# Batch 0's attention of a fused attention and max-out kernel, rewritten over both token halves

## The chip, the cores and the metric

The kernel runs on one core of one Trainium2 chip. The metric is device time in microseconds (us). The kernel before takes 320.83 us, the median of three runs (320.79 to 321.07). One execution was recorded by the hardware profiler; its own numbers are below.

## The reference

There are 8 batches of 8 heads, 1024 tokens and 64 values per head. Keys and values are first projected along the tokens, from 1024 rows to 64, by the matrices E and F. Then ordinary softmax attention follows, and its output goes through a max-out layer.

```
k_proj = np.einsum('ks,bhsd->bhkd', E, k)          # 64 x 64 per head
v_proj = np.einsum('ks,bhsd->bhkd', F, v)
scores = scale * np.matmul(q, k_proj.transpose(0, 1, 3, 2))
attn   = exp(scores) / sum(exp(scores))
x      = np.matmul(attn, v_proj)                   # -> 8192 tokens x 512
out    = np.maximum(x @ w1, x @ w2) @ w_out        # 512 -> 1024 -> 512
```

Inputs and output are float32. Because max(a, b) = max(a - b, 0) + b, the kernel computes `relu(x @ (w1 - w2)) @ w_out + x @ (w2 @ w_out)`. The difference `w1 - w2` is called `wd_sb`, the product `w2 @ w_out` is called `m_sb`.

## The kernel before, in words

Everything is float16 on the chip, with float32 sums. Each batch is cut into two token halves of 512 columns, and these are the units of work; there are 16. The order of the instructions is written out by hand: every engine works through its instructions in the order of the program text, and waits only where a semaphore says so. TensorE (PE) does the products, VectorE (DVE) and ScalarE (ACT) take results out of PSUM, GpSimd (POOL) issues the loads that change float32 to float16 on their way, and SyncE (SP) issues stores, transposing transfers and the first few plain loads.

The change touches the start of the kernel, that is batch 0 up to the point where the max-out products run without a break. The start of the program text is as follows.

- **Loads.** SP issues E (L80), then k of heads 0 and 1 as plain float32 (`kf_sb`, L81), then F (L82). POOL issues, each with a change of type: k of heads 2 and 3, then it makes the identity matrix, then q of heads 0 to 3, k of heads 4 to 7, q of heads 4 to 7 (all L102), v in four pieces of two heads (L102), and then the weights. The first four weight pieces (L124) are, in this order, rows 0 to 1 of the first 256 columns of `w2`, the same of `w1`, then rows 2 to 3 of `w2` and of `w1`. (A "row" here is one of four blocks of 128 model dimensions.) The rest of the weights follow (L133), `moe_w_out` (L137), then the next batches.
- **Turning E and F.** `step_eft(0)` and `step_eft(1)` (L158) transpose E and F on PE in float32, eight small transposes each, and copy them out as float16 `eft`.
- **Projections.** `step_kv` (L177) multiplies k by E and v by F; `step_kpt` (L273) transposes the projected keys, twice, into the upper and lower 64 partitions; `step_qt` (L298) transposes q.
- **Attention.** Heads are taken in two groups `g` of four, and tokens in two halves `j` of 256 columns per product. `step_sc` (L368) makes the scores and ACT their exponential; `step_dn` (L374) sums the exponentials on PE by a product with ones and ACT takes the logarithm; `step_inv` (L382) turns the logarithm into the reciprocal; `step_at` (L386) makes the products with the projected values on PE, and DVE multiplies them by the reciprocal into `xt_sb` (L399).
- **Fillers.** `warm(n)` (L144) issues n products of ones whose result nobody reads.
- **Max-out, first part.** `step_wd` (L494) subtracts `w2` from `w1` on DVE; `up_slots` (L471) multiplies `xt_sb` by it, four products of 512 columns for each of eight blocks and each token half (L479); `step_w2t` (L500) transposes `w2` on PE (L504) and ACT copies it out (L510). The products of `m_sb` follow (`m_steps`, L581), then a steady stretch of products to the end (L693 and L785).

PSUM has eight banks. Four are single ones, `mm_bank()`, given out in a rotating order kept in the list `turn`, or by number. The other four are two pairs, `att_banks()`, tag `att`, with two buffers that are given out in turn; a new pair may be written only when every reader of the pair two calls before has finished. The order around the last step of the start is

```
    step_at(t, 1, 0, True)
    u0, u1 = [*up_slots(t, 0)], [*up_slots(t, 1)]
    step_wd(0, 2, 4)
    step_at(t, 1, 1, True)
    for u in u0, u1:
        for x in u[0:2]:
            x(r1=2)
    step_w2t(0, True)
```

Here `step_at(..., True)` takes its results from an `att` pair, and so does `step_w2t(0, True)`: the pair that the transposes write is the one of `step_at(t, 1, 0)`, whose two multiplications (L399) stand ahead of `step_wd(0, 2, 4)` on DVE. The next slots are the second halves of the first two products, `u0[0](r0=2)` and `u0[1](r0=2)`, then `step_w2t(256, True)` into the pair of `step_at(t, 1, 1)`.

Of the kernel before, what the change touches and what calls it, by code (L numbers as in the profile page):

```python
# [16 lines left out]
def kernel(  # L17
# [55 lines left out]
    def big(n, dtype=FP16):  # L73
        return const.tile([128, 16384 // mybir.dt.size(dtype) // 2], dtype, tag=f"big{n}", name=f"big{n}")

    ef_sb = big(0, FP32)[0:KP, :].rearrange("k (i s) -> k i s", i=2)
    kf_sb = const.tile([128, 2048], FP32, tag="wo", name="kf_sb")[:, 0 : 2 * NC * D].rearrange(
        "p (h c d) -> p h c d", h=2, d=D
    )
    nc.sync.dma_start(out=ef_sb[:, 0, :], in_=E)  # L80
    nc.sync.dma_start(out=kf_sb, in_=k[0, 0:2].rearrange("h (p c) d -> p h c d", c=NC))  # L81
    nc.sync.dma_start(out=ef_sb[:, 1, :], in_=F)  # L82
# [27 lines left out]
    for h0 in (0, H // 2):  # L110
        for n, src in (("k", k), ("q", q)):
            load(tiles[0], n, src, 0, h0 + 2 * ((h0, n) == (0, "k")), h0 + H // 2)
            if (h0, n) == (0, "k"):
                ident = const.tile([128, 128], FP32)
                make_identity(nc, ident)
# [24 lines left out]
    nc.vector.memset(ones16, 1.0)  # L140
    junk = const.tile([1, 1], FP16)


    def warm(n, att=False):  # L144
        w_ps = att_banks()[:, 0, :] if att else mm_bank()
        for _ in range(n):
            nc.tensor.matmul(
                out=w_ps, lhsT=ones16[:, 0:128], rhs=ones16, start=True, stop=True
            )

    warm(8)
    ident16 = const.tile([128, 128], FP16)
    nc.vector.tensor_copy(out=ident16, in_=ident)


    eft = [const.tile([128, NC, KP], FP16, tag=f"eft{i}", name=f"eft{i}") for i in range(2)]

    def step_eft(i):  # L158
        eft_ps = mm_bank()
        for c in range(NC):  # L160
            nc.tensor.transpose(
                out=eft_ps[:, c * KP : (c + 1) * KP],
                in_=ef_sb[:, i].rearrange("k (p c) -> k c p", c=NC)[:, c, :],
                identity=ident[:KP, :KP],
            )
        eng = nc.scalar.copy if i else nc.vector.tensor_copy
        eng(out=eft[i].rearrange("p c k -> p (c k)"), in_=eft_ps)
# [9 lines left out]
    def step_kv(t, h0=0, h1=H, which="kv", att=False, dma=False, copy=nc.vector.tensor_copy):  # L177
        kv_ps = att_banks()[:, 0, :] if att else mm_bank(n=0 if dma else None)
        n = (h1 - h0) * D
        both = which == "v"  # L180
        nh = 2 if both else h1 - h0
        for h in range(0, h1 - h0, nh):
            for c in range(NC):
                for w in which:
                    i = "kv".index(w)
                    for r in range(2) if both else (i,):
                        nc.tensor.matmul(  # L187
                            out=kv_ps[r * KP : (r + 1) * KP, h * D : (h + nh) * D],
                            lhsT=eft[i][:, c, :],
                            rhs=t[w][:, h0 + h : h0 + h + nh, c, :],  # L190
                            start=(c == 0), stop=(c == NC - 1),
                        )
        zd = lambda ap: ap.rearrange("p (h d z) -> p h z d", d=D // 2, z=2)
        if "k" in which:
            eng = nc.vector.tensor_copy if which == "k" or dma else nc.scalar.copy
            kp = t["kp"][:, h0:h1]
            eng(out=kp[:, :, 0, :], in_=kv_ps[0:KP, 0:n].rearrange("p (h d) -> p h d", d=D))
        if both:
            copy(out=t["vp"][:, h0:h1], in_=zd(kv_ps[:, 0:n]))
        elif "v" in which:  # L200
            def finish_v():
                nc.vector.tensor_copy(out=t["vp"][KP:128, h0:h1], in_=zd(kv_ps[KP:128, 0:n]))
                if dma:
                    nc.vector.tensor_copy(out=kp[:, :, 1, :], in_=kp[:, :, 0, :])
                    step_kpt_dma(t)
                else:
                    step_vp(t, h0, h1)

            if att:
                return finish_v  # L210
            finish_v()
# [59 lines left out]


    def step_kpt(t, h0=0, h1=H, att=False):  # L273
        kpt_ps = att_banks(FP16)[:, 0, :] if att else mm_bank(FP16)
        for h in range(h0, h1):
            for r in range(2):
                nc.tensor.transpose(
                    out=kpt_ps[r * D : (r + 1) * D, (h - h0) * KP : (h - h0 + 1) * KP],
                    in_=t["kp"][:, h, 0, :],
                    identity=ident16[:KP, :KP],  # L280
                )
        nc.vector.tensor_copy(
            out=t["kpt"][:, h0:h1, :].rearrange("q h k -> q (h k)"),
            in_=kpt_ps[:, 0 : (h1 - h0) * KP],
        )
# [100 lines left out]
    def step_at(t, g, j, att=False, between=None):  # L386
# [9 lines left out]
        for o in range(2):  # L396
            if o and between is not None:
                between()
            nc.vector.tensor_tensor(  # L399
                out=x_out(t, g, j)[:, :, o, :],  # L400
                in0=at_ps[o].rearrange("q (z n) -> q z n", z=2),
                in1=ld[:, o, None, :].broadcast_to([128, 2, W]),
                op=ALU.mult,
            )

# [121 lines left out]
    T_sb = const.tile([128, 4, NG + NX, CH], FP16)  # L527
# [35 lines left out]
    def m_steps():  # L563
# [41 lines left out]
        def p5():  # L605
            st["s5"] = keep("pu", product(5, "Z", 3))
# [293 lines left out]
    step_eft(0)  # L900
    nc.vector.tensor_copy(out=t["k"][:, 0], in_=kf_sb[:, 0])
    nc.scalar.copy(out=t["k"][:, 1], in_=kf_sb[:, 1])
    warm(5)
    step_kv(t, 0, 4, "k")
    step_eft(1)
    step_kpt(t, 0, 4)
    warm(3)
    step_qt(t, 0, 4, 0, NI // 2)
    step_qt(t, 0, 4, NI // 2, NI)
    warm(2)  # L910
    step_sc(t, 0, 0)
    step_sc(t, 0, 1)
    warm(2)
    step_kv(t, 4, 8, "k")
    step_dn(t, 0, 0)
    warm(2)
    step_kpt(t, 4, 8)
    step_dn(t, 0, 1)
    step_inv(t, 0, 0)
    step_inv(t, 0, 1)  # L920
    warm(2)
    step_qt(t, 4, 4, 0, NI // 2)
    step_qt(t, 4, 4, NI // 2, NI)
# [222 lines left out]
```

## Time and profile before

| | |
|---|---|
| median of three runs | 320.83 us (320.79 to 321.07) |
| profiled execution, its own time | 321.09 us |
| its span, first to last instruction | 319.3 us |
| outside the span | 1.8 us |
| PE busy / DVE busy / ACT busy / POOL busy | 312.9 / 241.3 / 205.8 / 39.7 us |
| PE instructions (products) | 3920 |
| first max-out product (L479) starts | 23.48 us |
| first weight transposes (L504) start | 25.37 us |

The page counts an instruction as busy from its start to its end. Products of PE are pipelined, so the busy time of a group is not the sum of single durations. In the timeline a line gives the start, the length of a merged run of instructions, engine, line, operation, what it writes and reads, shapes, how many instructions, and in brackets the idle time of the engine ahead of it with what ended that. In the list of DMA issues the last number of a line is the time from issue to landing.

### The profile page before, as it was taken

What the parts mean: (1) busy time and instruction counts of PE and PEld (TensorE: products, weight loads), DVE (VectorE), ACT (ScalarE), POOL (GpSimd) and SP (SyncE); (2) the same over time, 40 slices, a digit from 0 to 9 for tenths busy, and PEclk for the clock granted to TensorE, in tenths of its full rate; (3) what the DMA queues carried; (4) which work ended last, traced back from release to release, by engine and by line L of the source; (5) the groups of instructions that cost most, each with busy time, mean ns of one, the idle gap of its engine ahead of it and who ended that gap; (6) DMA issues with size and microseconds to landing.
All of it is one profiled execution on the core that took longest, in us unless ns stands there. A gap on an engine that the chain in (4) does not pass through costs nothing.

```text
span 319.3 us, 9176 instructions
## 1 busy us (share of the span) xinstructions
PE 312.9 (98%) x3920; PEld 253.2 (79%) x3920; DVE 241.3 (76%) x434; ACT 205.8 (64%) x372; POOL 39.7 (12%) x63
## 2 busy tenths in 40 slices
PE   8989999999999999999999999999999999999996
PEld 3554588788887888788887888788887888888885
DVE  2356889787969696896969696996969696969683
ACT  2376742767776777477776777477776777765541
POOL 8269102003000300021000400030000000000000
PEclk9999999999999999999999999999999999999999
DMA  7999999999979899899999999889969231303124
GB/s 185 200 200 193 199 207 202 207 165 154 206 136 179 156 205 245 219 192 158 233 204 215 168 216 245 198 157 169 239 141 211 50 102 35 101 33 102 35 99 131
DMA packets 76424, 53.41 MB, mean 167 GB/s; under 512 B 29536, under 2 KB 76000, under 8 KB 76384
## 3 DMA queue, kind: packets, MB, share of 16 engines
q0 software_dynamic: 30688, 28.05, 56.2%
q1 hardware_dynamic: 45408, 24.58, 32.3%
q8 instruction: 30, 0.49, 0.6%
q10 hardware_dynamic: 288, 0.20, 0.2%
q14 instruction: 10, 0.08, 0.1%
HBM read 57.15 MB, written 16.78 MB: 232 GB/s over the span
## 4 chain that ended last, share of the span: by engine, by line
PE 92%; DMA 4%; ACT 1%; POOL 1%; DVE 1%; issue 0%; POOLq 0%; DVEq 0%
PE mm_ps L785 46%; PE mm_ps L693 27%; PE mm_ps L479 4%; DMA v_sb<-in_v_dram 4%; PE att_ps L344 3%; PE mm_ps L187 3%; PE mm_ps L332 3%; PE mm_ps L581 2%; PE att_ps L229 1%; PE mm_ps L303 1%; POOL k_sb L102 0%; POOL q_sb L102 0%; PE att_ps L504 0%; PE att_ps L332 0%; ACT ld_sb L384 0%
## 5 line engine op out<-in xcount | busy, mean ns | idle before, releaser
L667 ACT COPY p_sb<-mm_ps 128x512 f32<-128x512 f32 x179 | 101.7, 592 | 49.4 <-PE mm_ps L693 27.3
L785 PEld LDWEIGHTS <-big 128*128 128x128 f16 x768 | 73.5, 98 | 11.8 <-issue 3.6
L785 PE MATMUL mm_ps<-T_sb,big 128*128 128x256 f16 x576 | 77.0, 273 | 0.0
L708 DVE TENSOR_TENSOR gt_sb<-mm_ps,p_sb 128x512 f16<-128x512 f32 x56 | 38.5, 687 | 42.7 <-PE mm_ps L693 42.3
L693 PE MATMUL mm_ps<-big,big 128*128 128x256 f16 x336 | 50.4, 273 | 0.0
L693 PEld LDWEIGHTS <-big 128*128 128x128 f16 x448 | 43.8, 98 | 5.1
L785 PE MATMUL mm_ps<-wo_sb,gt_sb 128*128 128x256 f16 x256 | 42.8, 273 | 0.0
L785 PEld LDWEIGHTS <-gt_sb 128*128 128x128 f16 x376 | 35.6, 98 | 7.0 <-issue 3.0
L425 ACT ACTIVATE ex_sb<-mm_ps 128x512 f16<-128x512 f32 x50 | 27.2, 596 | 18.2 <-PE mm_ps L332 13.0
L693 PEld LDWEIGHTS <-wd_sb 128*128 128x128 f16 x336 | 32.9, 98 | 4.1
L693 PE MATMUL mm_ps<-xt_sb,wd_sb 128*128 128x256 f16 x224 | 33.0, 272 | 0.0
L454 DVE TENSOR_TENSOR xt_sb<-att_ps,ld_sb 128x1024 f16<-128x1024 f32 x26 | 31.7, 1218 | 0.2
L785 PE MATMUL mm_ps<-m_sb,xt_sb 128*128 128x256 f16 x128 | 24.4, 273 | 0.0
L711 DVE TENSOR_SCALAR gt_sb<-gt_sb 128x512 f16<-128x512 f16 (+1 forms) x60 | 22.7, 378 | 2.1
L815 DVE TENSOR_TENSOR o_sb<-mm_ps,p_sb 128x512 f32<-128x512 f32 x32 | 21.8, 682 | 2.8 <-ACT p_sb L839 2.0
L295 POOL COPY junk<-qt_sb 1x1 f16<-1x1 f16 x6 | 1.1, 177 | 176.2 <-DMA qt_sb<-q_sb 176.2
L653 DVE TENSOR_TENSOR big<-gt_sb 128x1024 f16<-128x1024 f16 x32 | 21.9, 683 | 0.0
L785 PE MATMUL mm_ps<-wo_sb,big 128*128 128x256 f16 x128 | 21.5, 273 | 0.0
L754 ACT ACTIVATE gt_sb<-mm_ps 128x512 f16<-128x512 f32 x28 | 16.8, 601 | 5.7 <-PE mm_ps L693 5.7
L785 PE MATMUL mm_ps<-T_sb,gt_sb 128*128 128x256 f16 x120 | 20.3, 273 | 0.0
L785 PEld LDWEIGHTS <-xt_sb 128*128 128x128 f16 x188 | 18.4, 98 | 2.1
L708 DVE TENSOR_TENSOR gt_sb<-p_sb 128x512 f16<-128x512 f32 x28 | 19.1, 682 | 0.7 <-ACT p_sb L667 0.6
(112 smaller groups left out, 434.7 us busy)
## 6 DMA issues: line engine op xcount, KB each, us to landing
out_dram<-o_sb SPq DMA_DIRECT2D x62, 256.0 KB, 2.7
k_sb<-in_k_dram POOLq DMA_DIRECT2D x7, 1024.0 KB, 10.4
v_sb<-in_v_dram POOLq DMA_DIRECT2D x7, 1024.0 KB, 17.0
q_sb<-in_q_dram POOLq DMA_DIRECT2D x5, 1024.0 KB, 23.9
q_sb<-in_q_dram POOLq DMA_DIRECT2D x6, 512.0 KB, 16.2
big<-in_moe_w_dram POOLq DMA_DIRECT2D x12, 128.0 KB, 6.3
v_sb<-in_v_dram POOLq DMA_DIRECT2D x4, 256.0 KB, 13.8
wo_sb<-in_moe_w_out_dram POOLq DMA_DIRECT2D x1, 1024.0 KB, 10.4
```

What stands on the lines that cost most here:

```text
L187: nc.tensor.matmul(out=kv_ps[r * KP : (r + 1) * KP, h * D : (h + nh) * D], lhsT=eft[i][:, c, :], rhs=t[w][:, h0 + h : h0 + h + nh, c, :], ...
L425: nc.scalar.activation(out=t["ex", g, j][:, e, :], in_=banks[e], func=ACTF.Exp, scale=scale)
L454: nc.vector.tensor_tensor(out=x_out(t, g, j).rearrange("q z o n -> q o z n"), in0=at_ps.rearrange("q o (z n) -> q o z n", z=2), in1=ld[:, ...
L479: nc.tensor.matmul(out=h_ps, lhsT=wd_sb[:, r, fb * 128 : (fb + 1) * 128], rhs=t["xt"][:, r, :, j * W : (j + 1) * W], start=(r == 0), stop= ...
L653: nc.vector.tensor_tensor(out=S(i), in0=S(0) if x is None else x, in1=y(), op=op)
L667: copy(out=x, in_=bank)
L693: nc.tensor.matmul(out=bank[:, m * W : (m + 1) * W], lhsT=w_[:, n_, (2 * d + m) * 128 : (2 * d + m + 1) * 128], rhs=a[:, n_, :], start=(n ...
L708: nc.vector.tensor_tensor(out=c_blk(j, c), in0=two(x), in1=two(y), op=ALU.add)
L711: nc.vector.tensor_scalar_max(ap, ap, 0.0)
L754: nc.scalar.activation(out=out, in_=in_, func=ACTF.Relu)
L785: nc.tensor.matmul(out=bank[i][:, 0:CH] if two_banks else bank[:, i * CH : (i + 1) * CH], lhsT=a(c)[:, i * 128 : (i + 1) * 128], rhs=w_(c) ...
L815: nc.vector.tensor_tensor(out=o_sb, in0=two(x), in1=two(y), op=ALU.add)
```

## The change

Only batch 0's path to its `xt_sb` changes; the rest of the program is the same text.

- E and F are loaded into the lower and upper 64 partitions of one tile, E by SP and F by ACT's queue. k of heads 0 to 3 is loaded as plain float32, two heads by each of the two queues, and changed to float16 on DVE and ACT. POOL no longer loads k of heads 2 and 3.
- E and F are changed to float16 together (`ef16`) and transposed together, eight transposes of 128 by 128. F is kept once as `eft[1]` and once doubled side by side (`fdup`), so that one product gives the projected values for both halves of the partitions.
- Scores, sums and value products run over both token halves at once, 512 columns each. The score products use 64 columns of weights instead of 32. The logarithm and the reciprocal of a group are one ACT instruction each, on `ld0`, which shares its memory with `T_sb`.
- The value products of group 0 (`step_at0`) go to the four single banks, with `step_wd(0, 0, 2)` ahead of the last of their four multiplications. Those of group 1 (`step_at1`) go to the two `att` pairs, one for each `o`, and their four multiplications, first `j` = 0 and then `j` = 1, all stand behind `step_wd(0, 2, 4)` on DVE.
- The rotating order of single banks is set to 2, 3, 1, 0 ahead of the max-out products, the first eight of these are ordered by row, and `p5` of `m_steps` uses bank 1 instead of 3.
- Fillers are float32 products of ones.

```diff
--- before.py
+++ after.py
-    ef_sb = big(0, FP32)[0:KP, :].rearrange("k (i s) -> k i s", i=2)
-    kf_sb = const.tile([128, 2048], FP32, tag="wo", name="kf_sb")[:, 0 : 2 * NC * D].rearrange(
-        "p (h c d) -> p h c d", h=2, d=D
+    ef_sb = big(0, FP32)[:, 0:S]
+    raw_sb = const.tile([128, 2048], FP32, tag="wo", name="raw_sb").rearrange(
+        "p (n h c d) -> p n h c d", n=2, h=2, d=D
     )
-    nc.sync.dma_start(out=ef_sb[:, 0, :], in_=E)
-    nc.sync.dma_start(out=kf_sb, in_=k[0, 0:2].rearrange("h (p c) d -> p h c d", c=NC))
-    nc.sync.dma_start(out=ef_sb[:, 1, :], in_=F)
+    nc.sync.dma_start(out=ef_sb[0:KP], in_=E)
+    nc.scalar.dma_start(out=ef_sb[KP:128], in_=F)
+    for n, queue in enumerate((nc.sync, nc.scalar)):
+        queue.dma_start(
+            out=raw_sb[:, n], in_=k[0, 2 * n : 2 * n + 2].rearrange("h (p c) d -> p h c d", c=NC)
+        )
...
-    for h0 in (0, H // 2):
-        for n, src in (("k", k), ("q", q)):
-            load(tiles[0], n, src, 0, h0 + 2 * ((h0, n) == (0, "k")), h0 + H // 2)
-            if (h0, n) == (0, "k"):
-                ident = const.tile([128, 128], FP32)
-                make_identity(nc, ident)
+    load(tiles[0], "q", q, 0, 0, H // 2)
+    ident16 = const.tile([128, 128], FP16)
+    make_identity(nc, ident16)
+    for n, src in (("k", k), ("q", q)):
+        load(tiles[0], n, src, 0, H // 2, H)
...
+    ones32 = opool.tile([128, 512], FP32, tag="o", name="ones32_sb")
+    nc.vector.memset(ones32, 1.0)
     junk = const.tile([1, 1], FP16)
 
 
-    def warm(n, att=False):
-        w_ps = att_banks()[:, 0, :] if att else mm_bank()
-        for _ in range(n):
+    def warm(*cols):
+        w_ps = mm_bank()
+        for n in cols:
             nc.tensor.matmul(
-                out=w_ps, lhsT=ones16[:, 0:128], rhs=ones16, start=True, stop=True
+                out=w_ps[:, 0:n], lhsT=ones32[:, 0:128], rhs=ones32[:, 0:n], start=True, stop=True
             )
 
-    warm(8)
-    ident16 = const.tile([128, 128], FP16)
-    nc.vector.tensor_copy(out=ident16, in_=ident)
+    warm(512, 256)
 
 
     eft = [const.tile([128, NC, KP], FP16, tag=f"eft{i}", name=f"eft{i}") for i in range(2)]
-
-    def step_eft(i):
-        eft_ps = mm_bank()
+    ef16 = opool.tile([128, S], FP16, tag="o", name="ef16_sb")
+    fdup = opool.tile([128, NC, 2, KP], FP16, tag="o", name="fdup_sb")
+
+    def step_eft():
+        ps_t = mm_bank(FP16)
         for c in range(NC):
             nc.tensor.transpose(
-                out=eft_ps[:, c * KP : (c + 1) * KP],
-                in_=ef_sb[:, i].rearrange("k (p c) -> k c p", c=NC)[:, c, :],
-                identity=ident[:KP, :KP],
+                out=ps_t[:, c * 128 : (c + 1) * 128],
+                in_=ef16.rearrange("q (p c) -> q c p", c=NC)[:, c, :], identity=ident16,
             )
-        eng = nc.scalar.copy if i else nc.vector.tensor_copy
-        eng(out=eft[i].rearrange("p c k -> p (c k)"), in_=eft_ps)
+        both = ps_t.rearrange("p (c i k) -> p c i k", c=NC, i=2)
+        nc.vector.tensor_copy(out=eft[0], in_=both[:, :, 0, :])
+
+        def finish():
+            nc.scalar.copy(out=fdup, in_=both[:, :, 1, None, :].broadcast_to([128, NC, 2, KP]))
+            nc.scalar.copy(out=eft[1], in_=both[:, :, 1, :])
+
+        return finish
...
+    def step_k0(t, h0, h1):
+        k_ps = mm_bank()[0:KP, 0 : (h1 - h0) * D]
+        for c in range(NC):
+            nc.tensor.matmul(
+                out=k_ps, lhsT=eft[0][:, c, :], rhs=t["k"][:, h0:h1, c, :],
+                start=(c == 0), stop=(c == NC - 1),
+            )
+        nc.vector.tensor_copy(
+            out=t["kp"][:, h0:h1],
+            in_=k_ps.rearrange("p (h d) -> p h d", d=D)[:, :, None, :].broadcast_to([KP, h1 - h0, 2, D]),
+        )
+
+    def step_kpt0(t, h0, h1):
+        kpt_ps = mm_bank(FP16)
+        for h in range(h0, h1):
+            nc.tensor.transpose(
+                out=kpt_ps[:, (h - h0) * KP : (h - h0 + 1) * KP],
+                in_=t["kp"][:, h].rearrange("k z d -> k (z d)"), identity=ident16[:KP, :KP],
+            )
+        nc.vector.tensor_copy(
+            out=t["kpt"][:, h0:h1, :].rearrange("q h k -> q (h k)"), in_=kpt_ps[:, 0 : (h1 - h0) * KP]
+        )
+
+    def step_v0(t, h0, h1, nh, copy):
+        v_ps = mm_bank()
         for h in range(0, h1 - h0, nh):
             for c in range(NC):
+                nc.tensor.matmul(
+                    out=v_ps[:, h * D : (h + nh) * D],
+                    lhsT=fdup[:, c].rearrange("p r k -> p (r k)"),
+                    rhs=t["v"][:, h0 + h : h0 + h + nh, c, :],
+                    start=(c == 0), stop=(c == NC - 1),
+                )
+        copy(out=t["vp"][:, h0:h1], in_=zd(v_ps[:, 0 : (h1 - h0) * D]))
...
+    ld0 = const.tile([128, 2, 2, HALF], FP32, tag="tsb", name="ld0_sb")
+
+    def step_sc0(t, g):
+        t["ps", g], t["ex", g] = [], []
+        for h in range(2):
+            sc_ps = att_banks()
+            for o in range(2):
+                for e in range(2):
+                    head, pos = 4 * g + 2 * h + e, D * (o ^ e)
+                    nc.tensor.matmul(
+                        out=sc_ps[pos : pos + D, e, :],
+                        lhsT=kpt_of(t, head, o),
+                        rhs=t["qt"][o * D : (o + 1) * D, head, :],
+                        start=True, stop=True,
+                    )
+            ex = soft.tile([128, 2, HALF], FP16, tag="soft", name="ex_sb")
+            nc.scalar.activation(out=ex, in_=sc_ps, func=ACTF.Exp, scale=scale)
+            t["ps", g].append(sc_ps)
+            t["ex", g].append(ex)
+
+    def tiles0(t, g, dst, weights):
+        for h in range(2):
+            for r in range(2):
+                rows = slice(r * KP, (r + 1) * KP)
+                for e in range(2):
+                    hh = 2 * h + e
+                    nc.tensor.matmul(
+                        out=dst(r ^ e)[hh * Z : (hh + 1) * Z, :],
+                        lhsT=weights(rows, hh), rhs=t["ex", g][h][rows, e, :],
+                        start=True, stop=True,
+                    )
+
+    def step_dn0(t, g):
+        dn_ps = t.pop(("ps", g))[0]
+        tiles0(t, g, lambda o: dn_ps[:, o, :], lambda rows, hh: ones16[rows, 0:Z])
+        nc.scalar.activation(out=ld0[:, g], in_=dn_ps, func=ACTF.Ln)
+
+    def step_inv0(g):
+        nc.scalar.activation(out=ld0[:, g], in_=ld0[:, g], func=ACTF.Exp, scale=-1.0)
+
+    def step_at0(t, between):
+        at_ps = []
+        for z in range(2):
+            at_ps.append([mm_bank() for _ in range(2)])
+            tiles0(t, 0, lambda o: at_ps[z][o], lambda rows, hh: vp_of(t, hh, rows, z))
+        for z in range(2):
+            for o in range(2):
+                if z and o:
+                    between()
+                nc.vector.tensor_tensor(
+                    out=t["xt"][:, z, o, :], in0=at_ps[z][o], in1=ld0[:, 0, o, :], op=ALU.mult
+                )
+
+    def step_at1(t):
+        at_ps = [att_banks() for _ in range(2)]
+        for z in range(2):
+            tiles0(t, 1, lambda o: at_ps[o][:, z, :], lambda rows, hh: vp_of(t, 4 + hh, rows, z))
+        for j in range(2):
+            for o in range(2):
+                cols = slice(j * W, (j + 1) * W)
+                nc.vector.tensor_tensor(
+                    out=t["xt"][:, 2:4, o, cols], in0=at_ps[o][:, :, cols],
+                    in1=ld0[:, 1, o, None, cols].broadcast_to([128, 2, W]), op=ALU.mult,
+                )
...
-    T_sb = const.tile([128, 4, NG + NX, CH], FP16)
+    T_sb = const.tile([128, 4, NG + NX, CH], FP16, tag="tsb", name="T_sb")
...
-            st["s5"] = keep("pu", product(5, "Z", 3))
+            st["s5"] = keep("pu", product(5, "Z", 1))
...
     t = tiles[0]
     new_attn(t)
     new_xt(t)
-    step_eft(0)
-    nc.vector.tensor_copy(out=t["k"][:, 0], in_=kf_sb[:, 0])
-    nc.scalar.copy(out=t["k"][:, 1], in_=kf_sb[:, 1])
-    warm(5)
-    step_kv(t, 0, 4, "k")
-    step_eft(1)
-    step_kpt(t, 0, 4)
-    warm(3)
-    step_qt(t, 0, 4, 0, NI // 2)
-    step_qt(t, 0, 4, NI // 2, NI)
-    warm(2)
-    step_sc(t, 0, 0)
-    step_sc(t, 0, 1)
-    warm(2)
-    step_kv(t, 4, 8, "k")
-    step_dn(t, 0, 0)
-    warm(2)
-    step_kpt(t, 4, 8)
-    step_dn(t, 0, 1)
-    step_inv(t, 0, 0)
-    step_inv(t, 0, 1)
-    warm(2)
-    step_qt(t, 4, 4, 0, NI // 2)
-    step_qt(t, 4, 4, NI // 2, NI)
-    warm(2)
-    step_sc(t, 1, 0)
-    step_kv(t, 0, 2, "v")
-    step_sc(t, 1, 1)
-    step_kv(t, 2, 4, "v")
-    step_dn(t, 1, 0)
-    step_dn(t, 1, 1)
-    step_inv(t, 1, 0)
-    step_inv(t, 1, 1)
-    step_at(t, 0, 0)
-    step_at(t, 0, 1, between=lambda: step_wd(0, 0, 2))
-    step_kv(t, 4, 8, "v", True, copy=nc.scalar.copy)
-    step_at(t, 1, 0, True)
+    nc.vector.tensor_copy(out=ef16, in_=ef_sb)
+    cast = lambda eng, h: eng(out=t["k"][:, h], in_=raw_sb[:, h // 2, h % 2])
+    cast(nc.vector.tensor_copy, 0)
+    finish_f = step_eft()
+    cast(nc.scalar.copy, 1)
+    cast(nc.scalar.copy, 2)
+    cast(nc.vector.tensor_copy, 3)
+    finish_f()
+    warm(512, 256)
+    step_k0(t, 0, 4)
+    warm(256)
+    step_kpt0(t, 0, 4)
+    warm(512)
+    step_qt(t, 0)
+    step_qt(t, 2)
+    step_sc0(t, 0)
+    step_k0(t, 4, 8)
+    step_dn0(t, 0)
+    step_inv0(0)
+    step_kpt0(t, 4, 8)
+    warm(256)
+    step_qt(t, 4)
+    step_qt(t, 6)
+    warm(128)
+    step_sc0(t, 1)
+    step_v0(t, 0, 4, 4, nc.vector.tensor_copy)
+    step_at0(t, lambda: step_wd(0, 0, 2))
+    step_dn0(t, 1)
+    step_v0(t, 4, 8, 2, nc.scalar.copy)
+    step_inv0(1)
     u0, u1 = [*up_slots(t, 0)], [*up_slots(t, 1)]
     step_wd(0, 2, 4)
-    step_at(t, 1, 1, True)
-    for u in u0, u1:
-        for x in u[0:2]:
-            x(r1=2)
+    step_at1(t)
+    turn.sort(key=(2, 3, 1, 0).index)
+    for r in range(2):
+        for u in u0, u1:
+            for x in u[0:2]:
+                x(r0=r, r1=r + 1)
     step_w2t(0, True)
```

More of the change, by code (lines that the diff above doesn't have):

```diff
@@ L174, in new_attn, with step_kv @@
         t["qt"] = qtp.tile([128, H, HALF], FP16, tag="qt", name="qt_sb")
-    def step_kv(t, h0=0, h1=H, which="kv", att=False, dma=False, copy=nc.vector.tensor_copy):
+    def step_kv(t, h0=0, h1=H, which="kv", att=False, dma=False):
         kv_ps = att_banks()[:, 0, :] if att else mm_bank(n=0 if dma else None)
         n = (h1 - h0) * D
-        both = which == "v"
-        nh = 2 if both else h1 - h0
+        for c in range(NC):
+            for i, w in enumerate("kv"):
+                nc.tensor.matmul(
+                    out=kv_ps[i * KP : (i + 1) * KP, 0:n],
+                    lhsT=eft[i][:, c, :],
+                    rhs=t[w][:, h0:h1, c, :],
+                    start=(c == 0), stop=(c == NC - 1),
+                )
+        kp = t["kp"][:, h0:h1]
+        nc.vector.tensor_copy(
+            out=kp[:, :, 0, :], in_=kv_ps[0:KP, 0:n].rearrange("p (h d) -> p h d", d=D)
+        )
+        nc.vector.tensor_copy(out=t["vp"][KP:128, h0:h1], in_=zd(kv_ps[KP:128, 0:n]))
+        nc.vector.tensor_copy(out=kp[:, :, 1, :], in_=kp[:, :, 0, :])
+        step_kpt_dma(t)
@@ new lines, in zd @@
+    def zd(ap):
+        return ap.rearrange("p (h d z) -> p h z d", d=D // 2, z=2)
+    def step_k0(t, h0, h1):
+        k_ps = mm_bank()[0:KP, 0 : (h1 - h0) * D]
+        for c in range(NC):
+            nc.tensor.matmul(
[6 more added lines that the diff above has]
+        )
@@ new lines, in step_kpt0 @@
+    def step_kpt0(t, h0, h1):
[5 more added lines that the diff above has]
+            )
+        nc.vector.tensor_copy(
+            out=t["kpt"][:, h0:h1, :].rearrange("q h k -> q (h k)"), in_=kpt_ps[:, 0 : (h1 - h0) * KP]
+        )
+    def step_v0(t, h0, h1, nh, copy):
+        v_ps = mm_bank()
@@ L182, in step_kv @@
         for h in range(0, h1 - h0, nh):
             for c in range(NC):
[L184 to L211, printed above, removed]
+                nc.tensor.matmul(
+                    out=v_ps[:, h * D : (h + nh) * D],
+                    lhsT=fdup[:, c].rearrange("p r k -> p (r k)"),
+                    rhs=t["v"][:, h0 + h : h0 + h + nh, c, :],
+                    start=(c == 0), stop=(c == NC - 1),
+                )
@@ L270, in vp_of @@
         return t["vp"][rows, head, z, :]
[L273 to L285, printed above, removed]
     def step_kpt_dma(t):
@@ new lines, in tiles0 @@
+    def tiles0(t, g, dst, weights):
[4 more added lines that the diff above has]
+                    hh = 2 * h + e
+                    nc.tensor.matmul(
+                        out=dst(r ^ e)[hh * Z : (hh + 1) * Z, :],
[6 more added lines that the diff above has]
+        nc.scalar.activation(out=ld0[:, g], in_=dn_ps, func=ACTF.Ln)
@@ new lines, in step_inv0 @@
+    def step_inv0(g):
[11 more added lines that the diff above has]
+                    out=t["xt"][:, z, o, :], in0=at_ps[z][o], in1=ld0[:, 0, o, :], op=ALU.mult
+                )
@@ new lines, in step_at1 @@
+    def step_at1(t):
[8 more added lines that the diff above has]
+                    in1=ld0[:, 1, o, None, cols].broadcast_to([128, 2, W]), op=ALU.mult,
+                )
```

## The prediction

> **What bounds the kernel now.** I read the page first, then the windows, then the timeline of the start. The page and the windows (time, then busy PE, PEld, DVE, ACT, POOL):
>
> ```profile
> span 319.3 us, 9176 instructions
> PE 312.9 (98%) x3920; PEld 253.2 (79%) x3920; DVE 241.3 (76%) x434; ACT 205.8 (64%) x372; POOL 39.7 (12%) x63
> PE 92%; DMA 4%; ACT 1%; POOL 1%; DVE 1%; issue 0%; POOLq 0%; DVEq 0%
> 50.00:300.00 250.00, 249.90 (x3237) 209.85 (x3232) 201.80 (x361) 172.78 (x319) 18.12 (x29) 1.00 0.88 167
> ```
>
> From 50 to 300 us PE is busy 249.90 of 250, and all its work there stays the same text. So the start can only move the moment at which PE begins to run without a break; the end moves by as much. The chain gives DMA 4%: that is the start. The timeline there:
>
> ```profile
> 4.84 2.84 POOL L102 DMA_DIRECT2D v_sb<-in_v_dram  x4
> 16.04 0.71 POOL L124 DMA_DIRECT2D big<-in_moe_w_dram  x1 [1.84 <-DMA q_sb<-in_q_dram]
> 18.41 0.48 PEld L187 LDWEIGHTS <-eft 128*64 128x64 f16 x16 [0.54 <-DMA v_sb<-in_v_dram]
> 20.65 0.63 PE L344 MATMUL mm_ps<-ex_sb,vp_sb 64*32 64x256 f16 x32
> 21.20 1.89 DVE L399 TENSOR_TENSOR xt_sb<-mm_ps,ld_sb 128x512 f16<-128x512 f32 x3 [0.91 <-PE mm_ps L344]
> 23.48 1.90 PE L479 MATMUL mm_ps<-xt_sb,wd_sb 128*128 128x512 f16 x8
> 23.94 1.28 DVE L399 TENSOR_TENSOR xt_sb<-att_ps,ld_sb 128x512 f16<-128x512 f32 x2
> 25.14 0.42 DVE L495 TENSOR_TENSOR wd_sb<-big,big 128x512 f16<-128x512 f16 x1
> 25.37 0.61 PE L504 MATMUL att_ps<-ident,big 128*128 128x128 f16 x8
> 25.47 1.28 DVE L399 TENSOR_TENSOR xt_sb<-att_ps,ld_sb 128x512 f16<-128x512 f32 x2
> 25.82 1.03 PE L479 MATMUL mm_ps<-xt_sb,wd_sb 128*128 128x512 f16 x4
> 26.90 0.61 PE L504 MATMUL att_ps<-ident,big 128*128 128x128 f16 x8
> ```
>
> See three things. Nothing of v's work starts before v lands (18.4). From 21.20 DVE has hardly a pause. And both groups of transposes (L504) start 0.15 us after a pair of multiplications ends: 23.94 + 1.28 = 25.22, then 25.37; 25.47 + 1.28 = 26.75, then 26.90. They wait for their PSUM pair. The weights' landing, and the DMA engines by windows (last two columns: share, GB/s):
>
> ```profile
> big<-in_moe_w_dram POOLq DMA_DIRECT2D x1, 128.0 KB, 8.9
> 2.00:3.00 1.00, 1.00 (x4) 0.32 (x3) 0.23 (x1) 0.03 (x1) 0.92 (x4) 1.00 0.80 193
> 3.00:4.00 1.00, 1.00 (x4) 0.30 (x3) 0.00 (x0) 0.00 (x0) 1.00 (x2) 1.00 0.98 258
> 7.00:8.00 1.00, 0.99 (x9) 0.72 (x8) 0.23 (x1) 0.00 (x0) 1.00 (x2) 1.00 1.05 155
> 8.00:12.00 4.00, 3.60 (x41) 2.45 (x38) 1.29 (x3) 0.59 (x1) 1.03 (x2) 1.00 1.20 195
> ```
>
> The first line is the issue at 16.04: the fourth weight piece lands at 16.04 + 8.9 = 24.94, just ahead of the subtraction at 25.14 that reads it. The engines carry one unbroken stream from 2 us on; loads that change type write half of what they read, so 195 GB/s written is 390 read.
>
> **The change part by part.** The sum is made against the profiled execution, 321.09 us (span 319.3 and 1.8 around it); the median is 0.26 below, so I add the difference to 320.83.
>
> *PE's products: nothing.* Scores were 64 products of 256 columns on eight array parts at once, and become 16 of 512 columns on four at once: 64 x 256 / 8 = 16 x 512 / 4 = 2048 columns one behind another. Sums (32 to 16) and values (64 to 32) keep eight parts, half the instructions at twice the columns. So the streamed time is equal; the row to scale is 32 products in 0.63. v's projection falls from 64 to 24 instructions, 2.36 us (0.64 + 0.64 + 1.08) to about 1.9 (eight of 256 columns at 1.06, as for k, and sixteen narrow ones at about 0.85). All lie ahead of 23.5 us, where PE waits for loads or for DVE anyway; without that cover they gain 0.5.
>
> *Casts and E, F.* Added: the cast of E and F, twice 0.50 (row 128x512); two more k casts (0.50 on DVE, 0.62 on ACT); `fdup`, about 1.0 on ACT (row of 128x1024). The copy of the projected keys grows from 0.42 to about 0.69, twice. Removed: 16 float32 transposes (1.10 + 1.09) for eight of 0.6 together, eight of the 16 key transposes (0.15), DVE's cast of the identity (0.23). q's 32 transposes and four copies stay. k of heads 0 to 3 goes into products at about 9 instead of 7.3. Cover: v lands at 18.4 to 19.0, while exponentials of group 1 end near 19 to 20 and only `step_dn0(1)` needs them. If the cover is gone the start slips by up to 1 us. Fillers in float32 cost about 0.85 for 512 columns (estimate from float32 transposes, 1.10 for eight of 64); they stand in waits for loads and DVE copies.
>
> *ACT.* Four logarithms (0.60) and four reciprocals (0.57) become two and two of about 1.0: 0.6 less, off the path. Its two new DMA issues (0.57 each, SP's row) stand ahead of a 1.28 us table load; ACT was idle until 5.92.
>
> *Queues.* POOL makes one issue less (0.83), so q and everything behind it is issued 0.75 earlier; the weight issues still wait for landings (1.84 idle ahead of 16.04), and lie far ahead of their data. SP keeps E and one k half. What counts is the stream's pace: call d the shift of all landings behind k and q. The six windows from 2 to 8 us read 193, 258, about 335, 408, 416 and 310 KB (type-changing loads counted double), 1.92 MB. Earliest: at 400 GB/s from 2.0 that takes 4.8 us and not 6, d = -1.2. Latest: 512 KB more in plain form at 258 instead of 390, d = +0.7. I take d = -0.6, as two queues feeding at once (5 to 7 us, some 410 read) outran one (193 to 335), but type-changing loads begin only near 4.7.
>
> The Trainium skill, "Trainium Kernel Development and Optimization", Key Constraints, speaks against that: issuing from several engines only saves issue time, as all queues run on the same 16 DMA engines. By it d would be about 0 and the time about 322.6; the share of 0.80 in the first window against 1.20 later leaves room, and so the sum goes by the windows.
>
> *The new order around `step_wd(0, 2, 4)`: the step that decides.* `step_at0`: v's second piece lands at 19.0 + d, products 1.06, copy 0.42, value products 0.57 with latency, hand-overs 0.15: first multiplication at 21.2 + d, as before. Three multiplications (1.89), subtraction, the fourth: about 23.9 + d. Then `step_wd(0, 2, 4)` waits on DVE for the fourth weight piece, 24.94 + d + 0.13 = 25.07 + d, and all four multiplications of `step_at1` are queued behind it. Before, two of the four stood ahead. The transposes `step_w2t(0, True)` now take the pair `o` = 0, read by the first and the third multiplication. By the rows the first ends a pair (25.14 to 26.75) 1.61 after the subtraction's start; a third adds 0.60: 2.21. So they start at 25.07 + 2.21 + 0.15 = 27.43 + d instead of 25.37: 2.06 + d later. PE has only eight products (L479), done at about 25.4, and then stands still, and everything behind it on PE with it.
>
> *What comes back.* The second transposes waited for their pair: from 25.82 to 26.90 is 1.08 for four products of 0.216, so 0.22 idle; now the pair is free 0.6 after the first one, with 1.3 of PE work between, so -0.22. `p5` on bank 1 no longer waits for the sum of `p2` (24 products from 41.21 to 43.96 where 24 x 0.11 are enough): -0.1. `p1` follows `u1[7]` on the bank of `u1[6]`, whose ACT copy just fits: +0.05. Shared memory of `ld0` and `T_sb` (first written at 37.8) and the three borrowed output buffers: nothing, their readers are done by 28.
>
> Sum: 2.06 - 0.6 - 0.22 - 0.1 + 0.05 = +1.2, so 322.0. With d from -1.2 to +0.7 it is +0.6 to +2.5.
>
> **The rivals.**
>
> *Faster: the load stream comes far earlier.* Landing-bound, the sum is 1.8 + d, so no change at d = -1.8 and faster by 0.2% from d = -2.4 (at -2.6: 320.0). For it: two plain queues from the first moment. Against: the windows from 2 to 8 us lack 1.2 in all, and v's landing and DVE's own chain (seven multiplications, two subtractions, 4.95 from the first to the freed pair) would bind next.
>
> *No change: the transposes are not held.* If their pair were free, PE would do them in the pause and go on when the first half of `step_at1` is there: 26.7 + d for what was at 25.82, less 0.3, so about 320.83 + 0.0 at d = -0.6. For it: nothing in the trace; against: the two 0.15 us gaps above.
>
> *Slower by more: a cold PE or a late front.* The first eight fillers took 3.60 us, 0.45 each, five later ones 1.25, 0.25 each, with the granted clock at 1.00 in both rows. If the new pause of some 1.5 us or the sparser fillers bring back the slow pace for the 3 us it lasted at the start, it costs 1.5: 323.5. Against: pauses of up to 0.57 us left no slow row behind. The Trainium skill, "TensorE: Matmul & The Clock Gate", Part 1 (The HAM clock gate), says it takes an idle window of about 3.4 us; by that it costs nothing, and no row here has such a pause.
>
> **How the numbers follow.** Forecast 0.67, faster 0.09, no change 0.10, slower by more 0.14. A difference under 0.2% (0.64 us) can't be told from none here. The forecast's early end (d near -1.2) lies within that: 0.05 of it goes to "same". Slower: 0.62 + 0.14 = 0.76. Range: 321.2 (d near -1.2 with a little more gained) to 323.1 (d = +0.5); it leaves out the faster case, half of the unchanged one and the cold PE.
>
> **What would show it.** Right: the first L504-type transposes start at about 26.8 with PE idle some 1.4 us ahead of them, released by the third multiplication of `step_at1`; the subtraction idle on DVE until the weights land; the fully busy stretch the same length as before; pieces landing 0.6 earlier. Wrong: the fourth weight piece at 23 us or earlier; no pause of PE ahead of the transposes; L479 products at 0.43 apart behind the pause; a last k cast later than 9.

## The result and the profile after

The changed kernel takes 323.82 us, the median of five runs (323.12 to 324.87), against 320.79 for the kernel before on the same chip (320.73 to 321.07). The ratio is 1.0098, 95% interval 1.0072 to 1.0124. So it is slower by about 3.0 us, where 1.2 was forecast; the sign was right, the size was not, and 323.82 lies above the range. The profiled execution is the slowest of the five: 324.87 us, span 323.1.

The page of the changed kernel, and its window of 250 us (time, then busy PE, PEld, DVE, ACT, POOL, granted clock, DMA share, GB/s):

```profile
span 323.1 us, 8847 instructions
PE 312.9 (97%) x3758; PEld 253.5 (78%) x3758; DVE 242.1 (75%) x435; ACT 206.9 (64%) x370; POOL 39.2 (12%) x62
54.00:304.00 250.00, 250.00 (x3239) 210.03 (x3236) 201.51 (x362) 172.72 (x320) 18.27 (x29) 1.00 0.85 163
```

PE has 162 instructions fewer and the same 312.9 us of busy time, and the long stretch is as dense as it was. All of the loss lies in the start. Its timeline, in order of time (start, length, engine, line, and in brackets the idle time ahead with what ended it):

```profile
1.35 0.86 ACTq L83 DMA_DIRECT2D raw_sb<-in_k_dram  x1
7.02 2.87 PE L151 MATMUL mm_ps<-ones_sb 128*128 128x512 f32 x4
10.29 0.62 ACT L984 CAST k_sb<-raw_sb 128x512 f16<-128x512 f32 x1 [3.00 <-DMA raw_sb<-in_k_dram]
10.96 1.86 PE L213 MATMUL mm_ps<-k_sb,eft 128*64 128x256 f16 x8 [1.08 <-ACT k_sb L984]
22.45 1.05 PE L237 MATMUL mm_ps<-v_sb,fdup_sb 128*128 128x256 f16 x8
24.57 1.89 DVE L473 TENSOR_TENSOR xt_sb<-mm_ps,ld_sb 128x512 f16<-128x512 f32 x3 [0.61 <-PE mm_ps L450]
26.67 1.06 ACT L462 ACTIVATE ld_sb<-ld_sb 128x1024 f32<-128x1024 f32 x1
27.31 0.41 DVE L578 TENSOR_TENSOR wd_sb<-big,big 128x512 f16<-128x512 f16 x1
27.77 2.48 DVE L484 TENSOR_TENSOR xt_sb<-att_ps,ld_sb 128x512 f16<-128x512 f32 x4
29.80 0.61 PE L587 MATMUL att_ps<-ident,big 128*128 128x128 f16 x8 [0.51 <-DVE xt_sb L484]
31.11 0.61 PE L587 MATMUL att_ps<-ident,big 128*128 128x128 f16 x8
```

The second half of the plain k load comes at 10.3 (1.35 plus the 8.9 below), and its casts wait for it. The eight products on k start at 10.96 instead of 7.28 and take 1.86 us instead of 1.06. The first multiplication of value products starts at 24.57 instead of 21.20, 3.37 later, and nothing ahead of it waits for v (L237). The forecast pause of PE ahead of the transposes (L587) is there, but only 0.51 us long.

The pause is not the whole cost of the new order. From the first multiplication to the first transposes it is 29.80 - 24.57 = 5.23 us, before 25.37 - 21.20 = 4.17: 1.06 more, although the subtraction (L578) finds its weights there. The transposes wait for the third of the four multiplications instead of the second, one of 0.6 us, and the four start at 27.77, when both the subtraction and ACT's reciprocal (L462, 26.67 + 1.06 = 27.73) have ended. The second transposes start 31.11 - 26.90 = 4.21 us later than before (3.37 + 1.06, less 0.22 that they no longer wait); 0.13 of it comes back at `p5`, and the profiled time is 324.87 - 321.09 = 3.8 longer.

Two issues in the list of DMA issues of the changed kernel (the last number is the time to landing), and its queues from 6 to 9.5 us (packets, MB, share of 16 engines; q0 is POOL's queue, q10 ACT's):

```profile
raw_sb<-in_k_dram ACTq DMA_DIRECT2D x1, 512.0 KB, 8.9
big<-in_moe_w_dram POOLq DMA_DIRECT2D x1, 128.0 KB, 8.4
q0 software_dynamic: 333, 0.34, 59.7%
q10 hardware_dynamic: 258, 0.51, 44.9%
```

From 6 us the k half shares the engines with POOL's q load, 258 packets beside 333. It also starts late: from 4.5 to 6 us its queue moves one packet, while SP's queue moves 0.45 MB, most of the other half. At that pace 0.51 MB alone from 6 us would have landed at about 7.7 (an estimate), so most of the lateness lies in the sharing; no run holds q back with this load kept. The fourth weight piece, issued at 16.67, lands at 25.1, before at 24.9. So the stream as a whole keeps its pace; only the order in it is worse.

### The profile page after: what moved, and what is told of

Its sections match the earlier page's. It is cut to its first block, busy times and chain, and to the rows that moved or that the text cites. A ratio compares the mean times of both kernels' runs of the same rounds, so it can differ in the third digit from the quotient of the medians.

```text
span 323.1 us, 8847 instructions
## 1 busy us (share of the span) xinstructions
PE 312.9 (97%) x3758; PEld 253.5 (78%) x3758; DVE 242.1 (75%) x435; ACT 206.9 (64%) x370; POOL 39.2 (12%) x62
## 4 chain that ended last, share of the span: by engine, by line
PE 93%; DMA 3%; DVE 2%; ACT 1%; issue 0%; ACTq 0%; DVEq 0%
PE mm_ps L868 46%; PE mm_ps L776 27%; PE mm_ps L562 4%; PE att_ps L361 3%; PE mm_ps L191 3%; DMA raw_sb<-in_k_dram 3%; PE mm_ps L349 2%; PE mm_ps L664 2%; PE att_ps L261 1%; PE mm_ps L151 1%; PE mm_ps L320 1%; PE mm_ps L237 1%; DVE qt_sb L325 1%; ACT ex_sb L440 1%; PE mm_ps L213 1%; DVE xt_sb L484 0%
## 5 line engine op out<-in xcount | busy, mean ns | idle before, releaser
L794 DVE TENSOR_SCALAR gt_sb<-gt_sb 128x512 f16<-128x512 f16 (+1 forms) x60 | 22.0, 366 | 2.1
```

The costliest lines, as they stand in the source:

```text
L794: nc.vector.tensor_scalar_max(ap, ap, 0.0)
```

## The experiments

Every kernel here computes the whole reference. Each median stands beside the kernel before on the same chip (320.85, 320.96, 321.24 and 321.04 in the four groups).

| kernel | median, us | ratio to before, 95% interval |
|---|---|---|
| changed kernel | 323.82 | 1.0072 to 1.0124 |
| the same again | 324.05 | 1.0053 to 1.0122 |
| k of heads 2, 3 by POOL | 322.82 | 1.0029 to 1.0073 |
| float16 fillers | 323.85 | 1.0063 to 1.0118 |
| float16 fillers until k is there | 323.52 | 1.0062 to 1.0092 |
| k by POOL and float16 fillers | 321.81 | 1.0018 to 1.0040 |
| those two, subtraction moved | 321.40 | 0.9984 to 1.0029 |
| those two, order mended | 320.67 | 0.9966 to 1.0008 |
| subtraction moved alone | 323.69 | 1.0056 to 1.0095 |
| all plain loads on SP | 328.76 | 1.0204 to 1.0277 |
| before, k load of the change | 323.47 | 1.0064 to 1.0095 |
| before, subtraction moved ahead | 321.64 | 0.9986 to 1.0030 |

### k of heads 2 and 3 by POOL, as before

```diff
-    for n, queue in enumerate((nc.sync, nc.scalar)):
-        queue.dma_start(out=raw_sb[:, n], ...)
+    nc.sync.dma_start(out=raw_sb[:, 0], in_=k[0, 0:2]...)
...
+    load(tiles[0], "k", k, 0, 2, H // 2)
     load(tiles[0], "q", q, 0, 0, H // 2)
...
-    cast(nc.scalar.copy, 2)
-    cast(nc.vector.tensor_copy, 3)
```

> The changed kernel, with k of heads 2 and 3 loaded as before: by POOL with a change of type, first in its queue. Two theories. LATE FRONT: the changed kernel loses because k of heads 2 and 3 lands at 10.3 us instead of 7.0 and because the float32 fillers run at half pace, so that the first multiplication of the value products begins at 24.6 instead of 21.2. FORECAST: it loses because all four multiplications of the second group stand behind the weight subtraction and the transposes wait for their PSUM pair. LATE FRONT expects k complete at about 7, but the fillers still end at about 9.9, so the k products start at 9.9 instead of 10.96: about 1.0 us faster than the changed kernel, 322.8. FORECAST expects no change, 323.8.

Measured 322.82 (321.56 to 323.42), 1.0 less than the changed kernel, the number that the late front gave. That is partly luck: two of the six runs lie at 321.56 and 321.72, the others from 322.57 to 323.42. The profiled execution is the fastest one; in it PE ran at full pace early, against the expectation, and no trace shows the slower runs. Its timeline:

```profile
6.68 1.51 PE L151 MATMUL mm_ps<-ones_sb 128*128 128x512 f32 x4
8.12 1.06 PE L213 MATMUL mm_ps<-k_sb,eft 128*64 128x256 f16 x8
20.51 1.89 DVE L473 TENSOR_TENSOR xt_sb<-mm_ps,ld_sb 128x512 f16<-128x512 f32 x3 [0.61 <-PE mm_ps L450]
```

The same four filler instructions that took 2.87 us in the changed kernel take 1.51 here. Between these two profiles, the fastest run here and the slowest of the changed kernel, the products on k start 2.84 us earlier and the first multiplication 4.06; the pace of PE adds to the load.

### Float16 fillers

```diff
-    def warm(*cols):   # float32 products of ones, n columns each
+    def warm(*cols):   # for each n: n // 128 float16 products of 512 columns
...
-    warm(512, 256)
+    warm(512, 512, 256)
```

> The changed kernel with float16 fillers: four products of 512 columns for each float32 one of 512, and ten ahead of the turning of E and F. LATE FRONT expects k still complete at 10.9, but its eight products in 1.06 us instead of 1.86 and shorter fillers behind them: about 1.2 faster than the changed kernel, 322.6. FORECAST expects no change, 323.8.

Measured 323.85: no gain, a miss. The four runs lie at 323.02 and 323.12, 324.59 and 324.62; the profile is of 324.59, and none shows the shorter ones. The expectation had the products on k right (10.83, eight in 1.09), but not what follows. The windows of this kernel (busy PE first after the time, granted clock third from the end):

```profile
9.00:10.00 1.00, 0.00 (x0) 0.00 (x0) 0.00 (x0) 0.00 (x0) 0.00 (x0) 1.00 1.20 241
12.00:15.00 3.00, 3.00 (x12) 0.99 (x11) 0.94 (x2) 0.18 (x1) 0.70 (x1) 0.50 1.24 206
```

PE runs out of fillers at 8.3 and idles until the products on k start at 10.8; the granted clock then is 0.50 from 12 to 15 us. The fillers and transposes behind k run at half pace, and the first multiplication comes at 24.24.

### Float16 fillers until k is there, and the changed kernel again

```diff
     finish_f()
-    warm(512, 256)
+    warm(512, 512, 512, 512, 256)   # 18 float16 products
```

> The changed kernel with float16 fillers, and with 18 instead of 6 of them ahead of the k products, so that PE has work from the turning of E and F until k is complete at about 10.8. If the fall to half pace behind an idle PE is part of the loss, the fillers and products behind k run at full pace, the value products' first multiplication comes at about 23.1 instead of 24.2, and the time falls by about 1.1 against the kernel with float16 fillers alone (323.85): 322.7. If the late landing alone is the loss, no change.

> The changed kernel once more, for its spread on one chip beside the others: 323.1 to 324.9 as before, and the profile slower where its first products on k take 1.86 us (half pace) than where they take 1.06.

Measured 323.52 (323.19 to 323.66) and, for the changed kernel, 324.05 in two clumps: 323.13 and 323.15, 324.94 and 325.19. With PE busy until k lands, none of the four runs lies near 325, and the first multiplication comes at 22.89. That is the late landing alone: 1.7 us behind the kernel before. The median fell by 0.3 against the float16 fillers (on another chip) and 0.5 against the changed kernel on the same chip, where 1.1 was expected; the shorter clumps of those two kernels lie at 323.0 to 323.2 already. That PE kept its pace in these shorter runs is likely, but no profile shows it. The profile of the changed kernel again, of the clump near 325 (324.94), shows the clock as well:

```profile
10.84 1.03 PE L213 MATMUL mm_ps<-k_sb,eft 128*64 128x256 f16 x8 [2.63 <-ACT k_sb L984]
13.00:16.00 3.00, 3.00 (x17) 1.78 (x17) 0.41 (x2) 0.00 (x0) 0.70 (x1) 0.56 1.24 207
```

Its products on k took 1.03 us, not 1.86, and yet it belongs to the longer clump, its first multiplication at 24.61; so that sign was wrong. Here PE reached full pace and lost it at about 12 us; in the first profile of the changed kernel it had not yet left the half pace of its first fillers. What decides is the pace in the whole stretch up to 16 us.

### Both edits

> Both edits together. LATE FRONT expects the k products at about 8.1, the first multiplication of the value products back at 21.2, bound by v's landing; what is left is then the forecast's term, the wait of the transposes for their pair, PE idle some 1.5 us ahead of them: about 322.6. If that wait costs nothing, 320.8. FORECAST alone, without a late front, expects 323.8.

Measured 321.81 (321.60 to 321.99), where 322.6 was expected. The timeline:

```profile
8.63 1.06 PE L212 MATMUL mm_ps<-k_sb,eft 128*64 128x256 f16 x8
20.84 1.89 DVE L472 TENSOR_TENSOR xt_sb<-mm_ps,ld_sb 128x512 f16<-128x512 f32 x3 [0.61 <-PE mm_ps L449]
24.30 0.42 DVE L577 TENSOR_TENSOR wd_sb<-big,big 128x512 f16<-128x512 f16 x1 [0.33 <-DMA big<-in_moe_w_dram]
24.64 2.48 DVE L483 TENSOR_TENSOR xt_sb<-att_ps,ld_sb 128x512 f16<-128x512 f32 x4
26.66 0.61 PE L586 MATMUL att_ps<-ident,big 128*128 128x128 f16 x8 [0.97 <-DVE xt_sb L483]
27.97 0.61 PE L586 MATMUL att_ps<-ident,big 128*128 128x128 f16 x8
```

This is the forecast's picture: DVE waits for the weights ahead of the subtraction, four multiplications stand behind it, and PE idles 0.97 us until the third has ended. The second transposes start 1.07 later than before; less 0.13 for `p5` that is 0.94; the medians differ by 0.96, the profiled times by 0.71. The weights landed at 24.2, 0.7 ahead of the kernel before, so the pause is shorter than expected. So of the 3.0 us lost, 2.0 go with these two edits, and the 1.0 that is left is the new order.

From the start of the products on k to the first multiplication it is 12.2 us here (8.63 to 20.84), and 12.2 with fillers until k is there (10.68 to 22.89). So the first multiplication follows k, and v's landing no longer covers anything. With k in products at 9, as the prediction had it, and PE at full pace, it would have come at 21.2, as before.

### The subtraction moved

```diff
-    step_wd(0, 2, 4)
-    step_at1(t)
+    step_at1(t, lambda: step_wd(0, 2, 4))   # called ahead of j = 1
```

> As the kernel with both edits (POOL's load of k, float16 fillers; 321.81 us), with the weight subtraction for rows 2 and 3 moved behind the first two of the four multiplications of the second group. FORECAST's term says that its last 1.0 us is the wait of the transposes for their pair: with the subtraction moved, the third multiplication ends about 0.4 earlier, PE idle ahead of the transposes falls from 0.97 to about 0.6: 321.4. If the wait is not what costs, no change against 321.81.

> The changed kernel with the weight subtraction for rows 2 and 3 moved behind the first two multiplications of the second group, all else as it is. LATE FRONT: by the time DVE comes to that subtraction (27.3 us) its weights have long landed (25.1), so that its place costs nothing and the time stays at 323.8. FORECAST, if it held in the changed kernel as it stands: about 0.4 faster, 323.4.

With both edits it gives 321.40, 0.41 less, as expected (on another chip; against each group's kernel before it is 0.52), and PE idles 0.55 instead of 0.97 there, with 0.21 more among the products ahead:

```profile
26.09 0.61 PE L588 MATMUL att_ps<-ident,big 128*128 128x128 f16 x8 [0.55 <-DVE xt_sb L485]
```

Alone in the changed kernel it gives 323.69. The two groups' kernels before differ by 0.45, and the intervals of the ratios overlap, so its time settles nothing. The trace says more:

```profile
26.31 1.29 DVE L486 TENSOR_TENSOR xt_sb<-att_ps,ld_sb 128x512 f16<-128x512 f32 x2 [0.38 <-ACT ld_sb L462]
28.68 0.61 PE L589 MATMUL att_ps<-ident,big 128*128 128x128 f16 x8 [0.85 <-DVE xt_sb L486]
```

The subtraction starts at 27.52 without a wait, its weights long there. But the multiplications still start 3.2 us after the first one (26.31 after 23.12; unmoved, 27.77 after 24.57), since they wait for ACT's reciprocal. Ahead of them the subtraction filled that wait; between them it makes the third multiplication later, and PE idles 0.85 instead of 0.51.

### The kernel before, with one part each

```diff
-    nc.sync.dma_start(out=kf_sb, in_=k[0, 0:2]...)
+    nc.sync.dma_start(out=kf_sb[:, 0:2], in_=k[0, 0:2]...)
+    nc.scalar.dma_start(out=kf_sb[:, 2:4], in_=k[0, 2:4]...)
```

In this kernel POOL's load of heads 2 and 3 is gone too, and two casts are added behind the plain load.

> The kernel before, with one part of the change alone: k of heads 2 and 3 loaded as plain float32 by the ACT queue and cast on ACT and DVE, and not by POOL. LATE FRONT expects these two heads to land at about 10, the score products some 2.6 us later and the time up by about 2.1: 322.9. FORECAST, which gave loads of either kind the same place in the stream, expects 320.8 to 321.1.

The other part alone, the order on DVE:

```diff
+    step_wd(0, 2, 4)
     step_at(t, 1, 0, True)
-    step_wd(0, 2, 4)
     step_at(t, 1, 1, True)
```

> The kernel before with the forecast's step alone: the weight subtraction for rows 2 and 3 moved ahead of the two multiplications of step_at(1, 0), nothing else changed. FORECAST: these multiplications then wait on DVE for the fourth weight piece, the pair comes free at about 26.75 and not 25.22, the first transposes start some 1.5 us later, of which 0.22 comes back at the second transposes: 322.1. If order on DVE around that subtraction is cheap, 320.8 to 321.0.

The load alone costs the kernel before 2.6 us (323.47, expected 322.9), though by another detail than expected: here the ACT queue's k half goes first and E lands late, so that PE turns E at 7.36 instead of 4.99 and the products on k run at half pace:

```profile
7.36 1.06 PE L161 MATMUL mm_ps<-ident,big 64*128 64x64 f32 x8 [2.31 <-DMA big<-in_E_dram]
10.18 1.92 PE L187 MATMUL mm_ps<-k_sb,eft 128*64 128x256 f16 x8
```

So this run does not test the late landing of heads 2 and 3 by itself; it does show that this front is dear without the new order, the first multiplication at 24.06.

The order on DVE alone costs it 0.7 in the median (321.64, 321.32 to 322.20), where 1.3 was expected, and with this chip's spread the interval holds 1. The profiled run, 322.12, one of the two longest of ten, shows the forecast term at its full size:

```profile
25.09 0.42 DVE L495 TENSOR_TENSOR wd_sb<-big,big 128x512 f16<-128x512 f16 x1 [1.00 <-DMA big<-in_moe_w_dram]
26.86 0.61 PE L504 MATMUL att_ps<-ident,big 128*128 128x128 f16 x8 [1.41 <-DVE xt_sb L399]
```

### All plain loads on one queue

```diff
-    nc.scalar.dma_start(out=ef_sb[KP:128], in_=F)
-    for n, queue in enumerate((nc.sync, nc.scalar)):
-        queue.dma_start(
+    nc.sync.dma_start(out=ef_sb[KP:128], in_=F)
+    for n in range(2):
+        nc.sync.dma_start(
```

> The changed kernel with all four plain loads on SP's queue, in the order E, F, k of heads 0 and 1, k of heads 2 and 3. If two plain queues share one stream, as the trace of the changed kernel suggests (0.50 MB from 2 to 4 us by two queues, 0.45 by one before), the last k half lands at about 10.3 again and the time stays at 323.8. If two queues do outrun one, as the prediction took it, it lands later and the time rises by 0.5 or more.

Measured 328.76, 7.5 us above before and 4.9 above the changed kernel (3.1 between the profiled times): a miss for the shared stream as I had put it. The k halves land at 10.1 and 12.9:

```profile
12.91 0.62 ACT L984 CAST k_sb<-raw_sb 128x512 f16<-128x512 f32 x1 [2.13 <-DMA raw_sb<-in_k_dram]
```

From 4 to 6 us POOL's queue moves 303 packets and SP's 32, from 6 to 9.5 it is 358 to 282. The fourth weight piece lands at 24.1, no later than elsewhere. From 2 to 4 us one queue moves 0.46 MB here, two moved 0.50. So a second queue does not speed the stream by much; it decides how much of it the plain loads get once POOL's loads run, and one queue with three transfers ahead of the last gets it later. Why SP's third load was not under way by 5 us, and ACT's second in the changed kernel not by 6, is not shown.

### The order mended

The kernel with both edits, without one filler, and with four moves: the projected values of heads 0 and 1 ahead of the last scores and those of heads 2 and 3 behind them, the first subtraction behind all four multiplications of group 0, and the second one between the two PSUM pairs:

```diff
-    step_sc0(t, 1)
-    step_v0(t, 0, 4, 4, nc.vector.tensor_copy)
+    step_v0(t, 0, 2, 2, nc.vector.tensor_copy)
+    step_sc0(t, 1)
+    step_v0(t, 2, 4, 2, nc.vector.tensor_copy)
...
-        for j in range(2):
-            for o in range(2):
+        for o in range(2):
+            if o:
+                between()                  # step_wd(0, 2, 4)
+            for j in range(2):
```

> The changed kernel with both edits, and with its order mended: the value products of the second two heads alone behind the last scores, the first subtraction behind all four multiplications of group 0, the second one between the two pairs of multiplications of group 1 taken pair by pair, so that the first pair of PSUM comes free after two of them. If late front and pair wait are all that the change lost, it is at least level with the kernel before: 320.2 to 320.5, with half the attention instructions worth nothing by themselves. If 512-column products cost something of their own, 321 or more.

Measured 320.67 against 320.96, level within the interval. The first multiplication is at 19.71, 1.5 us ahead of the kernel before, and it brings almost nothing, because the weights are not there:

```profile
19.71 2.48 DVE L470 TENSOR_TENSOR xt_sb<-mm_ps,ld_sb 128x512 f16<-128x512 f32 x4 [0.57 <-ACT ex_sb L439]
22.98 0.42 DVE L578 TENSOR_TENSOR wd_sb<-big,big 128x512 f16<-128x512 f16 x1 [0.78 <-DMA big<-in_moe_w_dram]
```

So the whole loss can be had back without giving up the 512-column products, and half the instructions bring nothing that can be measured. A small cost or gain of their own could hide behind the weights' landing.

## Why the prediction was wrong

- **The bound, and PE's products at nothing:** right as far as can be seen. The window of 250 us stays full, PE's busy time is the same, and the mended kernel is level.
- **"Casts and E, F", the step that failed.** It put k into products at about 9 and let v's landing cover that, with "up to 1 us" if the cover were gone. The products came at 10.96, after a last cast at 10.29, one of the prediction's own signs of being wrong, and the cover was gone: the first multiplication slipped by 3.4 us in the profile. About 1.7 of that is the late landing (22.89 with PE kept busy, against 21.2), the rest mostly half pace (13.6 us from the products on k to it, against 12.2).
- **"Queues".** I followed the total and a single shift d for all landings, and took two queues to outrun one. From 2 to 4 us two queues moved 0.50 MB and one 0.45, so the rule that the prediction cites from the Trainium skill ("Trainium Kernel Development and Optimization", Key Constraints) held, and d was about 0 for the weights (25.07 against 24.94). What I had not priced is the order: q was issued on POOL ahead of everything, and from 6 us moved more packets than the k half that the products wait for, which itself had started late.
- **The decisive step, the wait for the PSUM pair:** the mechanism is right. PE idles 0.97 us with the front mended, 1.41 in the kernel before with the order alone, 0.51 in the changed kernel, where PE itself came 3.9 later. There the weights were not waited for, and yet the new order cost 1.06 us from the first multiplication to the transposes. With the front mended the transposes start 1.29 later than before (1.46 forecast), and 321.81 is near the forecast of 322.0. That its weights land 0.7 earlier, as the forecast's d of -0.6 had it, is luck, since the loads are others.
- **"ACT".** The prediction put the logarithms and reciprocals off the path. Group 1's reciprocal stands behind the copy of the projected values on ACT and ends, at 27.73, together with the subtraction: it is on the path, and it is why moving the subtraction alone brought nothing.
- **What comes back:** right for `p5`: 24 products from 45.42 to 48.04, 2.62 us instead of 2.75. The second transposes no longer waited, 0.22 as forecast (1.29 later at the first, 1.07 at the second, with both edits).
- **The rivals.** "A cold PE or a late front" is what happened, with 0.14 of the chance, and it named 323.5. Of its two reasons the pause behind the value products did not bring it; the sparser fillers may be part of it, since PE never left the half pace of its first fillers in one profile, and lost its pace behind a gap of 2.6 us in the other. The larger part, the wait for k, stood only in its name. The rival of a load stream that comes far earlier fell: nothing landed 1.8 us sooner.

## What to carry to other kernels

When loads are moved between queues, price the landing of the first thing that the chain waits for, not the total of the stream: here 512 KB took 8.9 us to land instead of 5.8 (half the written bytes), behind another load of its queue and beside one that is needed later. A filler that ends before the late input comes may not hold PE's pace: two of four runs were 1.5 us longer than the others, and none of four with fillers up to that input. And the idle time of PE ahead of a wait is not the whole cost of an order: 0.51 us of it stood for 1.06, and moving the subtraction was worth 0.4 us only where it waited for its weights.

## What the runs showed of the hardware that I had not expected

- With float16 fillers, PE idle for 2.5 us (8.3 to 10.8) was followed by a granted clock of 0.50 for 3 us and more, beginning about a microsecond after work had set in again; in the kernel before with the load of the change, idle for 2.3 us was followed by 0.50 from 9 to 12 us. The Trainium skill, "TensorE: Matmul & The Clock Gate", Part 1 (The HAM clock gate), speaks of an idle window of about 3.4 us; here a shorter idle stretch was enough.
- The times of one kernel fall into clumps: the changed kernel's second set lies at 323.13, 323.15, 324.94 and 325.19 (in its first set 323.37 and 323.82 lie between). That whether PE loses its pace changes from run to run is the likely reason; only one run of each set was profiled.
- In the first profile of the changed kernel PE works at half pace from its first filler at 2.0 (2.93 us for four that take 1.51 at full pace) until about 14 us (products on k 1.86 against 1.06), while the granted clock in the rows reads 1.00. Ahead of the first change of the clock, only the length of the instructions shows it.
